# Fused retention and gated feed-forward, one core: the operand sums of the first seven-product tile in another order and on one engine

## Chip, core and metric

The kernel runs on one core of a Trainium2 chip. The core has a matrix engine (TensorE, PE in the profile, with its weight loads as PEld), VectorE (DVE), ScalarE (ACT), GpSimd (POOL) and SyncE (SP), which here only issues DMAs. They run side by side and wait for each other by semaphores. The metric is the time of one execution in microseconds (us) on the device.

## What is computed

Eight batches of eight heads, 576 positions, head size 64. Retention is attention without a softmax, with a decay for each head; its output is then the input of a feed-forward block whose gate is h * cos(h):

```python
scores = scale * np.matmul(q, k.transpose(0, 1, 3, 2))
Dmat = np.where(rel >= 0, gamma[:, None, None] ** rel[None, :, :], 0.0)
attn = np.matmul(scores * Dmat, v)              # (8, 8, 576, 64)
x = attn.transpose(0, 2, 1, 3).reshape(4608, 512)
h = x @ w_in                                    # (4608, 2048)
out = (h * np.cos(h)) @ w_out                   # (4608, 512)
```

## The kernel before

**Tokens and tiles.** The 4608 tokens are cut twice. Retention works on 36 groups of 128 tokens (g). The feed-forward part works on ten tiles of 512, 256, 256 and then seven times 512 tokens (n); tile 3 is the first of the seven (`S7 = 3`), it starts at token 1024, and groups 12 to 15 are prepared for tile 4 while tile 3 runs.

**Retention of a group.** `load` (L105) has SP fetch q, k and v of a group into five buffers each. `prep` (L131) has GpSimd multiply q and k by powers of the decay (L140) and cast v (L155). `transposes` (L163) has SP transpose the result by DMA (L166, into qkT). `scores` (L186) makes q times k on TensorE for one group in a PSUM tile of two banks, tagged "a" or "b", and VectorE multiplies it by the causal mask into `ret` (L206). `states` (L247) multiplies k by v for the state that is carried from group to group; VectorE adds it to the state so far (L284, L286), ScalarE or VectorE casts it (L277). `attn_out` (L292) adds the group's own part (L332) and the carried part (L318) in bank "m", and ScalarE copies that to the next tile's input xT (L349).

**Feed-forward, first half.** `mm1` (L353) makes one block of h on TensorE (L364) in a PSUM tile "a", "b" or "m". ScalarE makes the cosine (L372), VectorE the product gT (L373). In tile 3 a block is 4 of the 16 slices of 128 hidden units by 256 tokens, so there are 8 blocks; `blocks` (L763 to L766) has their order: the first 256 tokens with slices 0, 4, 8, 12, then the second 256 tokens with the same. The later tiles have blocks of 2 slices by 512 tokens.

**Feed-forward, second half.** From tile 3 on, gT times w_out is a 2 x 2 product of quarters with seven instead of eight multiplications (`mm2_seven`, L507). `product` (L469) makes each from 16 matmuls (L497), in the order 1, 2, 6, 4, 7, 5, 3. Products 1, 2 and 4 read gT itself. Products 5, 6, 7 and 3 read sums gs5, gs6, gs7, gs3 of quarters of gT (L437), where gs6 is made from gs5 and gs3 from gs6. Each sum has 8 slices; a sum over 4 of them is an instruction of 128x1024, one over 8 of 128x2048. gs5, gs6 and gs3 are made on VectorE, gs7 on GpSimd in pieces of 2 slices (L435). `sums_after` (L444) puts some of them behind a block of `mm1`; `late_sums` (L463) makes the rest between products. The results are copied (L521) and added (L517) and stored by SP (L527); the adds and stores that a product leaves behind wait in the list `pend` until the next `flush`. A store calls `feed` (L579), which lets GpSimd, SP and the loads go on with later groups.

**Order around the change.** The order of instructions on each engine is written out by hand; an engine works through its own in order. In tile 3, retention work stands ahead of three of the products (`at`, L818 to L823): ahead of product 6 the `flush` and the scores of groups 12 and 13 (`scores2`, L734, banks "a" and "b"); ahead of product 5 `unit7` (L750) with states in bank "st", the output of groups 12 and 13 and the scores of 14 and 15; ahead of product 3 `unit7` with states in bank "b" and the output of groups 14 and 15. After product 1 VectorE makes the rest of gs5 and all of gs6 (`late_sums(n, (5, 6))`, L546), and after the scores ahead of product 6 all of gs3 (L541). `states` has a form `apart` (L254) for a bank "b", in which the two groups' states lie in the two banks of the tile. Tile 4 begins with blocks in the banks a, b, m.

Of the kernel before, what the change touches and what calls it, by code (L numbers as in the profile page):

```python
# [17 lines left out]
def kernel(  # L18
# [16 lines left out]
    nc = tc.nc  # L35
# [21 lines left out]
    S7 = 3  # L57
# [189 lines left out]
    def states(gs, bank="st"):  # L247

        gs = [g for g in gs if g < NG and g % PER != PER - 1]
        if not gs:
            return lambda: (lambda *_: None)
        apart = bank == "b"  # L254
        if apart:
            two = psum.tile([P, 2, 2, HG, D], F32, tag=bank, name="st")
            ps = two[:, :, 0]
        else:
            ps = psum.tile([P, len(gs), HG, D], F32, tag=bank, name="st")
        for x, g in enumerate(gs):  # L260
            qks, vb, qkT, qT = tiles["a", g]
            vs = v_odd[:, g // PER % 2] if g % PER == MIX else vb
            for hg in range(HG):
                for he in range(2):
                    nc.tensor.matmul(  # L265
                        ps[he * D : he * D + D, x, hg, :],
                        lhsT=qks[:, 1, 2 * hg + he, :],
                        rhs=vs[:, head(he, hg), :],
                        start=((apart or x == 0) and hg == 0),
                        stop=((apart or x + 1 == len(gs)) and hg == HG - 1),  # L270
                        skip_group_check=True,
                    )

        def copy(run=nc.vector.tensor_copy):
            for g in gs:
                s, sb = tiles.pop(("s32", g)), blocks4[g % 4]
                run(sb, s)  # L277
                tiles["sb", g + 1] = sb

        def add():  # L280
            for x, g in enumerate(gs):
                s = stp.tile([P, HG, D], F32, tag="s32", name="s32")
                if g % PER in (0, MIX):
                    nc.vector.tensor_copy(s, ps[:, x])  # L284
                else:
                    nc.vector.tensor_tensor(out=s, in0=ps[:, x], in1=tiles["s32"], op=ALU.add)  # L286
                tiles["s32"] = tiles["s32", g] = s
            return copy

        return add  # L290
# [129 lines left out]
    def g_sum(n, x, e0, e1):  # L420

        gT = tiles["g", n]

        def quarter(r, c):
            return gT[:, c * E2 : (c + 1) * E2, r * 256 : (r + 1) * 256]

        if ("gs", n, x) not in tiles:
            tiles["gs", n, x] = sump.tile([P, E2, 256], BF16, tag=f"gs{x}", name=f"gs{x}")
        a, b, op_ = {
            5: lambda: (quarter(1, 0), quarter(1, 1), ALU.add),  # L430
            6: lambda: (tiles["gs", n, 5], quarter(0, 0), ALU.subtract),
            7: lambda: (quarter(0, 0), quarter(1, 0), ALU.subtract),
            3: lambda: (quarter(0, 1), tiles["gs", n, 6], ALU.subtract),
        }[x]()
        eng, step = (nc.gpsimd, 2) if x == 7 else (nc.vector, e1 - e0)  # L435
        for e in range(e0, e1, step):
            eng.tensor_tensor(  # L437
                out=tiles["gs", n, x][:, e : e + step],
                in0=a[:, e : e + step],
                in1=b[:, e : e + step],  # L440
                op=op_,
            )

    def sums_after(n, i):  # L444

        if n == S7:
            if i < 2:
                w_sums(7, i * 4, i * 4 + 4)
            elif i in (4, 5):
                g_sum(n, 7, i % 4 * 4, i % 4 * 4 + 4)  # L450
            elif i == 6:
                g_sum(n, 5, 0, 4)
            return
        for x, e0, e1 in {
            2: ((7, 0, 4),),
            3: ((5, 0, 4),),
            4: ((6, 0, 4), (7, 4, 6)),
            5: ((3, 0, 4),),
            6: ((5, 4, 6), (7, 6, E2)),
        }.get(i, ()):  # L460
            g_sum(n, x, e0, e1)

    def late_sums(n, xs):  # L463
        for x in xs:
            first_part = n == S7
            e0 = {5: 4 if first_part else 6}.get(x, 0 if first_part else 4)
            g_sum(n, x, e0, E2)

    def product(n, x):  # L469
# [37 lines left out]
    def mm2_seven(n, at):  # L507

        s0 = starts[n] // P
        pend = []  # L510

        def flush():
            while pend:
                pend.pop(0)()

        def add(out_, in0, in1):
            return lambda: nc.vector.tensor_tensor(out=out_, in0=in0, in1=in1, op=ALU.add)  # L517

        def copied(tag, x):
            t = op.tile([P, 2, N2], F32, tag=tag, name="ot")  # L520
            nc.scalar.copy(t, tiles["all", x])  # L521
            return t

        def store(t, r, c, s):
            def go():
                r0 = starts[n] + r * 256
                nc.sync.dma_start(  # L527
                    out[r0 : r0 + 256, c * N2 : (c + 1) * N2].rearrange("(j p) c -> p j c", p=P),
                    t,
                )  # L530
                feed(s)

            return go

        for x in (1, 2, 6, 4, 7, 5, 3):
            if x in at:
                at[x](flush, pend)
            else:
                flush()
            if x == 6:  # L540
                late_sums(n, (3,))  # L541
            parts = product(n, x)
            if x == 1:
                c11 = copied("a", 1)
                if 2 not in at:
                    late_sums(n, (5, 6))  # L546
            elif x == 2:
                pend[:0] = [add(c11, c11, tiles["all", 2]), store(c11, 0, 0, s0)]
            elif x == 6:
                u1 = copied("b", 1)  # L550
            elif x == 4:
                c21 = copied("c", 4)
            elif x == 7:
                c22 = copied("d", 1)
                pend += [add(c21, c21, tiles["all", 1]), store(c21, 1, 0, s0 + 1)]
            elif x == 5:
                pend += [
                    add(c22, c22, tiles["all", 5]),
                    add(u1, u1, tiles["all", 5]),
                    store(c22, 1, 1, s0 + 2),  # L560
                ]
            elif n < last:
                pend += [add(u1, u1, tiles["all", 3]), store(u1, 0, 1, s0 + 3)]
                flush()
            else:
                flush()
                for (j, c0, c1), ps in zip(parts, tiles["o", 3]):
                    add(u1[:, j, c0:c1], ps, u1[:, j, c0:c1])()
                    r0 = starts[n] + j * P
                    nc.sync.dma_start(out[r0 : r0 + P, N2 + c0 : N2 + c1], u1[:, j, c0:c1])  # L570
# [189 lines left out]
    for n, w in enumerate(widths):  # L760

        if n in (0, 3):
            halves = [(h, et) for et in range(0, ET, 4) for h in range(2)]  # L763
            if n == 3:
                halves.sort()
            blocks = [(et, half * 256, 256) for half, et in halves]  # L766
        elif n == 1:
            blocks = [(et, half * P, P) for half in range(2) for et in (0, 8)]
        else:
            m = 1024 // w  # L770
            blocks = [(et, 0, w) for et in range(0, ET, m)]
            if n > S7:
                blocks = [(e + k * E2, 0, w) for e in range(0, E2, m) for k in range(2)]
# [14 lines left out]
        g = starts[n] // P + w // P  # L788
# [12 lines left out]
        elif n == 1:  # L801
            todo = pair(6, "ab", 16, 27)
        elif n == 2:
            todo = [(11, lambda: scores2(g)), (25, lambda: unit(g, "m", soon=True))]
            late += [lambda: unit(g + 2, "b", False)]
        else:
            at = {}
            if n + 1 < len(widths):

                def sums_then(then):  # L810
                    late_sums(n, (5, 6))
                    then()

                at = {
                    2: lambda then, off: unit7(g, "st", True, lambda: sums_then(then), off),
                    5: lambda then, off: unit7(g + 2, "st", True, then),
                }
                if n in (3, 4):  # L818
                    at = {
                        6: lambda then, off: (then(), scores2(g)),  # L820
                        5: lambda then, off: unit7(g, "st", True, then),
                        3: lambda then, off: unit7(g + 2, "b", n > 3, then),
                    }  # L823
            mm2_seven(n, at)
            continue
# [43 lines left out]
```

## Time and profile before

| | |
|---|---|
| median of 3 runs | 301.47 us (300.87 to 301.82) |
| the profiled execution | 301.3 us |
| its span, first to last instruction | 299.6 us |
| mean granted TensorE clock | 0.991 |
| TensorE busy | 286.9 us (96% of the span) |
| VectorE busy | 215.1 us (72%) |
| ScalarE busy | 134.1 us (45%) |
| GpSimd busy | 138.9 us (46%) |
| moved by DMA | 50.29 MB, mean 168 GB/s |

A row of the timeline tells start, length, engine, line, operation, tiles written and read, and shapes; a number in brackets is how long the engine stood idle before it, and who ended that. Rows of one kind that follow each other are merged (x16). Two rows of one engine can overlap by about 0.08 us, as an instruction's end is pipelined with the next one's start. A window row has the stretch, each engine's busy time in it with its number of instructions, the granted clock as a share of full speed, the DMA engines' busy share and GB/s. In the waits list a row has the total, the number of waits and the longest.

### The profile page before, as it was taken

The page shows a single profiled execution, that of the slowest core. Times are in us where ns is not written, and L with a number is a line of the kernel's source. Part 1 is how long each engine was busy: PE and PEld are TensorE (multiplying, and loading weights), DVE is VectorE, ACT ScalarE, POOL GpSimd, SP SyncE. Part 2 cuts the span into 40 slices and gives each one's busy share as a digit, 9 for nine tenths or more (in the row PEclk, how much of TensorE's full clock was granted, in tenths as well). Part 3 has the DMA queues.
Part 4 walks back from the last instruction along what each step waited for, and adds up shares of the span by engine and source line. Part 5 has one row for each costly group of instructions (what it writes and reads, how often), then busy time and mean ns, then how long its engine had stood idle before and what let it go on. Part 6 is the DMA issues. An engine that isn't in the chain of part 4 may idle for free.

```text
span 299.6 us, 7314 instructions
## 1 busy us (share of the span) xinstructions
PE 286.9 (96%) x3105; PEld 196.5 (66%) x3105; DVE 215.1 (72%) x262; ACT 134.1 (45%) x163; POOL 138.9 (46%) x151
## 2 busy tenths in 40 slices
PE   7899999999999878999999999999999999999994
PEld 3478647848478757547854785488548854884584
DVE  6776717664568986599678966896689669925943
ACT  3556333515245314553355542644364445525620
POOL 2750067436345797473863791379238113101410
PEclk9999999999999979999999999999999999999998
DMA  8999999999999999997999999996960250011013
GB/s 210 214 210 207 209 217 194 218 210 237 202 170 227 209 242 222 201 233 165 213 216 247 199 218 206 194 234 160 209 117 3 79 135 0 31 51 63 0 37 106
DMA packets 154305, 50.29 MB, mean 168 GB/s; under 512 B 140832, under 2 KB 153248, under 8 KB 154272
## 3 DMA queue, kind: packets, MB, share of 16 engines
q1 hardware_dynamic: 149504, 45.10, 78.9%
q0 software_dynamic: 4224, 4.19, 8.4%
q8 instruction: 24, 0.39, 0.6%
q10 hardware_dynamic: 544, 0.52, 0.5%
q14 instruction: 9, 0.07, 0.1%
HBM read 36.70 MB, written 9.44 MB: 154 GB/s over the span
## 4 chain that ended last, share of the span: by engine, by line
PE 54%; DVE 5%; ACT 1%; issue 0%; DVEq 0%
PE h L364 25%; PE o L497 24%; DVE gT L373 2%; PE ov L332 1%; PE sc L194 1%; PE st L265 1%; PE ov L318 1%; DVE gs L437 1%; DVE ot L517 1%; DVE ret L206 1%; ACT cosh L372 0%; DVE s L286 0%; ACT ot L521 0%; DVEq L864 0%; DVEq L517 0%
## 5 line engine op out<-in xcount | busy, mean ns | idle before, releaser
L364 PE MATMUL h<-xT,w_in_sb 128*128 128x512 bf16 (+2 forms) x832 | 127.6, 314 | 0.8 <-DVE xT L349 0.7
L373 DVE TENSOR_TENSOR gT<-h,cosh 128x1024 bf16<-128x1024 f32 x72 | 88.0, 1223 | 37.3 <-ACT cosh L372 37.2
L372 ACT ACTIVATE cosh<-h,half_pi 128x1024 f32<-128x1024 f32 x72 | 80.2, 1114 | 66.7 <-PE h L364 66.0
L364 PEld LDWEIGHTS <-w_in_sb 128*128 128x128 bf16 x832 | 75.7, 98 | 50.0 <-issue 1.3
L437 POOL TENSOR_TENSOR gs<-gT 128x512 bf16<-128x512 bf16 x28 | 36.0, 1293 | 78.7 <-DVE gT L373 78.7
L140 POOL TENSOR_TENSOR qks<-fq,gq 128x512 bf16<-128x512 f32 x32 | 35.0, 1092 | 48.8 <-DMA fq<-in_q_dram 48.6
L497 PEld LDWEIGHTS <-gs 128*128 128x128 bf16 x456 | 44.0, 99 | 9.4 <-DVE gs L437 3.1
L140 POOL TENSOR_TENSOR qks<-fk,gk 128x512 bf16<-128x512 f32 x35 | 38.6, 1104 | 9.7 <-DMA fk<-in_k_dram 9.1
L206 DVE TENSOR_TENSOR ret<-sc,tri 128x1024 bf16<-128x1024 f32 x32 | 38.1, 1218 | 2.7 <-PE sc L194 2.7
L521 ACT COPY ot<-o 128x512 f32<-128x512 f32 x28 | 16.4, 586 | 45.7 <-PE o L497 44.6
L497 PEld LDWEIGHTS <-gT 128*128 128x128 bf16 x336 | 32.5, 98 | 6.0 <-DVE gT L373 0.6
L497 PE MATMUL o<-ws,gs 128*128 128x256 bf16 x224 | 28.4, 283 | 2.9 <-DVE gs L437 2.9
L517 DVE TENSOR_TENSOR ot<-ot,o 128x512 f32<-128x512 f32 x34 | 22.6, 682 | 11.0 <-ACT ot L521 7.9
L381 PE MATMUL o<-w_out_sb,gT 128*128 128x512 bf16 x128 | 30.1, 380 | 0.0
L497 PE MATMUL o<-w_out_sb,gs 128*128 128x256 bf16 (+1 forms) x232 | 26.8, 269 | 0.0
L497 PE MATMUL o<-w_out_sb,gT 128*128 128x256 bf16 x224 | 26.5, 273 | 0.3 <-DVE gT L373 0.3
L155 POOL CAST vb<-fv 128x512 bf16<-128x512 f32 x32 | 20.9, 652 | 8.3 <-DMA fv<-in_v_dram 7.7
L349 ACT CAST xT<-ov 128x1024 bf16<-128x1024 f32 (+1 forms) x18 | 16.5, 917 | 14.7 <-PE ov L318 12.6
L381 PEld LDWEIGHTS <-gT 128*128 128x128 bf16 x128 | 11.8, 98 | 12.5
L437 DVE TENSOR_TENSOR gs<-gT 128x512 bf16<-128x512 bf16 (+1 forms) x20 | 13.4, 672 | 0.3
L497 PE MATMUL o<-ws,gT 128*128 128x256 bf16 x112 | 13.4, 272 | 0.0
L391 ACT COPY ot<-o 128x512 f32<-128x512 f32 x8 | 4.7, 588 | 17.8 <-PE o L381 17.8
(69 smaller groups left out, 178.9 us busy)
## 6 DMA issues: line engine op xcount, KB each, us to landing
out_dram<-ot SPq DMA_DIRECT2D x35, 256.0 KB, 3.7
fk<-in_k_dram SPq DMA_DIRECT2D x32, 256.0 KB, 4.9
fv<-in_v_dram SPq DMA_DIRECT2D x32, 256.0 KB, 5.2
fq<-in_q_dram SPq DMA_DIRECT2D x30, 256.0 KB, 4.7
w_in_sb<-in_moe_w_in_dram POOLq DMA_DIRECT2D x4, 512.0 KB, 9.1
w_out_sb<-in_moe_w_out_dram POOLq DMA_DIRECT2D x4, 512.0 KB, 16.3
fq<-in_q_dram SPq DMA_DIRECT2D x8, 128.0 KB, 3.7
fk<-in_k_dram SPq DMA_DIRECT2D x8, 128.0 KB, 4.4
```

The lines of the kernel that those rows point to most:

```text
L140: eng.tensor_tensor(out=qks[:, m].rearrange("p (b a) d -> p a b d", a=2), in0=f.rearrange("p (a b) d -> p a b d", a=2), in1=by[:, c, :].re ...
L155: nc.gpsimd.tensor_copy(vb, fv)
L206: nc.vector.tensor_tensor(out=ret.rearrange("p a b i -> p (a b) i"), in0=ps.rearrange("p a b i -> p (a b) i"), in1=mask.unsqueeze(1).to_br ...
L349: evac(tiles["x", n][:, :, t0 : t0 + len(gs) * P], ps.rearrange("p c x i -> p c (x i)"))
L364: nc.tensor.matmul(ps[:, j, :], lhsT=w_in_sb[:, dg, (et + j) * P : (et + j + 1) * P], rhs=xT[:, dg, c0 : c0 + w], start=(dg == 0), stop=(d ...
L372: nc.scalar.activation(cosh, ps, ACTF.Sin, bias=half_pi, scale=1.0)
L373: nc.vector.tensor_mul(gT[:, et : et + m, c0 : c0 + w], ps, cosh)
L381: nc.tensor.matmul(ps, lhsT=gT[:, et, tsi * P : (tsi + 1) * P], rhs=w_out_sb[:, et, :], start=(et == 0), stop=(et == ET - 1),)
L437: eng.tensor_tensor(out=tiles["gs", n, x][:, e : e + step], in0=a[:, e : e + step], in1=b[:, e : e + step], op=op_,)
L497: nc.tensor.matmul(dst[i], lhsT=lhs[:, e, j * P : (j + 1) * P], rhs=rhs[:, e, c0:c1], start=(fresh and e == 0 and (i == 0 or len(parts) > 2)),
L517: return lambda: nc.vector.tensor_tensor(out=out_, in0=in0, in1=in1, op=ALU.add)
L521: nc.scalar.copy(t, tiles["all", x])
```

## The change

It touches tile 3 (and, in one function, the states' banks):

- the second 256 tokens' blocks are made in the order of slices 0, 8, 4, 12 instead of 0, 4, 8, 12;
- gs7 of tile 3 is made on VectorE, its first half behind the fifth block, its second half ahead of the scores that precede product 6; in the later tiles it stays on GpSimd;
- the first half of gs5 is made behind the sixth block instead of the seventh, the first half of gs6 behind the seventh; the second halves of both are made after product 1, where before the second half of gs5 and all of gs6 were made;
- gs3 of tile 3 goes to the next `flush`, ahead of product 4, instead of standing ahead of product 6; it is still one instruction;
- the states ahead of product 3 of tile 3 are made in bank "a" instead of "b", with the two groups apart as in "b".

```diff
-        apart = bank == "b"
+        apart = bank in "ab"
...
-        eng, step = (nc.gpsimd, 2) if x == 7 else (nc.vector, e1 - e0)
+        eng, step = (nc.gpsimd, 2) if x == 7 and n > S7 else (nc.vector, e1 - e0)
...
-            elif i in (4, 5):
-                g_sum(n, 7, i % 4 * 4, i % 4 * 4 + 4)
-            elif i == 6:
-                g_sum(n, 5, 0, 4)
+            elif i in (4, 5, 6):
+                g_sum(n, {4: 7, 5: 5, 6: 6}[i], 0, 4)
...
-            e0 = {5: 4 if first_part else 6}.get(x, 0 if first_part else 4)
+            e0 = 0 if first_part and x == 3 else 6 if x == 5 and not first_part else 4
...
-            if x == 6:
+            if x == 6 and n > S7:
                 late_sums(n, (3,))
...
-                halves.sort()
+                halves.sort(key=lambda u: (u[0], u[0] * (u[1] % 8), u[1]))
...
+                def before_p6(n, then, off):
+                    then()
+                    if n == S7:
+                        late_sums(n, (7,))
+                    scores2(g)
+                    if n == S7:
+                        off.append(lambda: late_sums(n, (3,)))
...
-                        6: lambda then, off: (then(), scores2(g)),
+                        6: lambda then, off: before_p6(n, then, off),
                         5: lambda then, off: unit7(g, "st", True, then),
-                        3: lambda then, off: unit7(g + 2, "b", n > 3, then),
+                        3: lambda then, off: unit7(g + 2, "ab"[n > S7], n > S7, then),
```

## Prediction, made before the changed kernel had run

> **What bounds the kernel now.** I read the page first, then the waits, then the timelines of tile 3 (span 80 to 122), then the granted clock by stretch. The page says that TensorE is the bound:
>
> ```profile
> PE 286.9 (96%) x3105; PEld 196.5 (66%) x3105; DVE 215.1 (72%) x262; ACT 134.1 (45%) x163; POOL 138.9 (46%) x151
> ```
>
> So only time in which TensorE stands, or runs slowly, can be won. The waits list names two such places in reach of the diff:
>
> ```profile
> PE o L497 <- DVE gs L437: 2.9, 1, 2.9
> ...
> PE st L265 <- DVE ret L206: 1.2, 2, 0.8
> ```
>
> The first is product 6 of tile 3, which waits for the operand sum gs6. TensorE's timeline has both (start, length, and in brackets the idle time before):
>
> ```profile
> 103.19 0.64 PE L194 MATMUL sc<-qkT 64*64 64x128 bf16 x32
> 106.73 3.50 PE L497 MATMUL o<-ws,gs 128*128 128x256 bf16 x16 [2.90 <-DVE gs L437]
> ...
> 117.93 0.44 PE L265 MATMUL st<-vb,qks 128*64 128x64 bf16 x16 [0.79 <-DVE ret L206]
> ```
>
> Product 6 then takes 3.33 (106.73 to product 4's start at 110.06) where the product after it takes 1.75 (110.06 to 111.81). The stretches say why (columns: length, TensorE busy, ..., granted clock):
>
> ```profile
> 103.18:106.59 3.41, 0.65 (x33) 0.48 (x32) 3.38 (x2) 0.00 (x0) 3.41 (x3) 1.00 1.31 222
> 106.59:110.00 3.41, 3.27 (x16) 2.34 (x17) 3.41 (x5) 0.00 (x0) 3.41 (x4) 0.50 1.26 262
> 110.00:113.41 3.41, 3.41 (x33) 3.06 (x32) 1.21 (x1) 1.17 (x2) 3.41 (x4) 1.00 1.27 251
> ```
>
> After a stretch of 3.41 us with only 0.65 busy, the next ran at a clock of 0.50. The stall's whole price is 2.90 + (3.33 - 1.75) = 4.48 us. The Trainium skill, in TensorE: Matmul & The Clock Gate, "Why this matters for your kernels", puts the fall of the clock behind idle gaps over about 3 us; the gap here is 2.90, and the trace has the fall all the same. By that sentence the 1.58 would not belong to this gap, and the forecast's gain of 2.4 would be about 0.8; the measured clock decides.
>
> Why gs6 is late stands in VectorE's and GpSimd's timelines:
>
> ```profile
> 100.46 1.45 DVE L437 TENSOR_TENSOR gs<-gT 128x1024 bf16<-128x1024 bf16 x1
> 101.83 1.21 DVE L373 TENSOR_TENSOR gT<-h,cosh 128x1024 bf16<-128x1024 f32 x1
> 103.08 1.50 DVE L437 TENSOR_TENSOR gs<-gT 128x1024 bf16<-128x1024 bf16 x1
> 104.62 2.05 DVE L437 TENSOR_TENSOR gs<-gs,gT 128x2048 bf16<-128x2048 bf16 x1
> ```
>
> ```profile
> 96.90 1.04 POOL L140 TENSOR_TENSOR qks<-fk,gk 128x512 bf16<-128x512 f32 x1 [0.16 <-DMA fk<-in_k_dram]
> 99.64 0.61 POOL L155 CAST vb<-fv 128x512 bf16<-128x512 f32 x1 [1.70 <-DMA fv<-in_v_dram]
> 100.21 5.38 POOL L437 TENSOR_TENSOR gs<-gT 128x512 bf16<-128x512 bf16 x4
> 105.55 2.02 POOL L140 TENSOR_TENSOR qks<-fq,gq 128x512 bf16<-128x512 f32 x1
> ```
>
> The same VectorE sum (128x1024) takes 0.68 at 133.05, where GpSimd is idle at its start. Beside GpSimd's four pieces of gs7 it takes 1.45 and 1.50, and GpSimd's multiplication at 105.55 takes 2.02 instead of 1.04 beside gs6. They take turns: a sum that meets a running GpSimd instruction starts when that one ends and then needs about 0.55 (1.08 for the double size). The multiplications by cos (1.21 to 1.23) show no such thing.
>
> **The change part by part.** Names: gT4 to gT7 are the four multiplications of the second half, a and b a sum's halves.
>
> *Order of blocks.* Same blocks, same banks, same 1.75 pitch of TensorE. Cost nothing; it lets gs5a follow the second of them instead of the third.
>
> *Sums.* GpSimd loses gs7 (5.38); VectorE gains gs7a and gs7b (0.68 each alone, up to 1.6 behind a GpSimd instruction). GpSimd does not fill the hole: its next load, fq of group 16, is issued at 99.64 and lands 3.6 later (103.2); fk lands at 104.6, fv at 105.7, fq and fk of group 17 at 107.0 and 108.2. VectorE's queue then, with steps of 1.17 to 1.25 per multiplication and about 0.6 per sum: gT4 95.71; gs7a from 96.97, behind GpSimd's 96.90 to 97.94, until 98.5; gT5 to 99.6; gs5a from 99.66, behind the cast that ends at 100.25, until 100.8; gT6 to 101.9; gs6a, GpSimd idle, to 102.7; gT7 to 103.8; gs5b from 103.84, behind group 16's fq (103.35 to 104.4), until 104.9; gs6b behind fk (until 105.8), until 106.4. TensorE: product 2 ends at 103.2, scores of the first group run, those of the second need gT7's bank (103.9, a wait of 0.4); product 6's first half runs 104.2 to 105.1 on gs6a, then waits 1.3 for gs6b. That the halves are waited for apart is taken from product 7, whose weight loads already follow GpSimd's four pieces one by one; were it not so, 0.9 more would go. Product 6 ends at 107.3 instead of 110.06: 2.8 won of 4.48. The one near tie is at 96.9: if gs7a goes first (0.07 us decide), gs5a misses the cast too, gs6b ends near 103.9 and all 4.48 is won.
>
> *gs7b and gs3 behind.* After gs6b stand the add of c11 (0.60), gs7b (0.6), two masks (2.3) and gs3 (1.2): about 111.1. Product 7 needs gs7b at about 109.9, it is there by 107.7 (108.7 behind a GpSimd instruction). The state adds, next in the queue, become ready at 111.3. No DMA moves: the store of c11 and the loads and transposes fed with it stand on SP ahead of these sums, before and after. So this part costs nothing, with 0.2 to spare; each further wait for GpSimd (1.0) would move the adds and the masks behind them.
>
> *States in bank a.* They wait for the mask of bank a, 1.14 earlier than that of b; but attn_out, next on TensorE, needs the second mask after 0.5 more. Of the wait of 0.79 some 0.3 remains: 0.5 won. Tile 4's first block needs that bank back after product 3 (1.85): hidden. So tile 4 starts 3.3 earlier, at 117.7.
>
> *What is late next.* Two things. First, tile 4: GpSimd's preparation of groups 20 and 21 is tied to loads (123.18 to 129.2) and does not move, while VectorE's sums do. Each meets GpSimd once more often; a meeting costs up to 1.0, VectorE has no slack there (1.14 + 0.60 of a pitch of 1.73), and tile 4's first product already waits 0.27 for gT6. Played through with the same turn-taking, gT6 ends at 134.1 instead of 136.6: 2.5 left of 3.3, and for 1.8 to 2.5 at the start about 1.3. Second, transposes of group 23:
>
> ```profile
> 160.48 1.06 SPq L527 DMA_DIRECT2D out_dram<-ot  x1
> 161.64 1.39 SPq L166 DMA_TRANSPOSE qkT<-qks  x1
> ...
> DMA to landing us min/median/max: 5.0/5.0/5.0
> ```
>
> SP's queue is full without a hole from 99 to 178: the store at 160.48 carries data that was added by 151.2. So that transpose still lands at 161.64 + 5.0 = 166.6, and its scores now start at 169.46 (second half of the scores at 169.20). Beyond 2.8 us TensorE would wait there. Later ones have 4 us or more, and after 178 SP waits for VectorE and moves along.
>
> **Sum.** 2.8 + 0.5 - 0.9 (tile 4) = 2.4, under the cap of 2.8. The profiled execution took 301.3 (span 299.6), so 298.9; the runs' median is 301.47, so **299.1**.
>
> The Trainium skill, in Perfetto Trace Analysis, "Optimizing Scalar/DVE Operations", warns that moving work between GPSIMD and VectorE might not help, as they share a port. The rows agree that they block each other, but the piece of 5.38 becomes two of 0.68; by that sentence alone only the bank's 0.5 would be won.
>
> **The rivals.**
> 1. *Half the clock again, or more turns lost.* In the case above TensorE is busy about 1.7 of a stretch of 3.41; the trace shows 0.65 leading to the half clock and 2.62 (116.83 to 120.24) not, so 1.7 is open. With it product 6's rest and product 4 cost up to 1.7 more; 1.6 to 1.8 is won at tile 4's start, 1.3 after it: 300.2.
> 2. *Everything is won.* gs7a goes first, and group 23's transpose lands earlier, as DMA finds other gaps: 4.48 less 0.3: 297.3. Against it: SP's full queue.
> 3. *The change does not do it:* the halves are waited for whole, and gs3 pushes the masks back by as much as was won; the wait only moves to L206 and to tile 4. Near 301.2.
> 4. *Slower: VectorE's queue.* If a GpSimd instruction stood ready at each of the seven sums (1.5 to 1.6 each, gs3 2.1), gs6b would end at 108.5, gs3 at 115.1, against 114.1 for the state adds now, and the mask before product 3 would be 1.0 later than today: about 302.4. It decides once the sums lose over some 5 us in all. Against it: GpSimd has no data between 100.25 and 103.2.
>
> **Chances and range.** Forecast (298.6 to 299.7) 0.52; rival 1 (299.8 to 300.5) 0.24; rival 2 0.09; rival 3 0.10; rival 4 0.05. Faster by over 0.3% (0.9 us, about what a measurement here can tell from no change): 0.85; within: 0.10; slower: 0.05. The range leaves out rival 4, most of 2 and most of 3: 298.2 to 300.7.
>
> **What would show it.** Right: no GpSimd row at L437 before tile 4; product 6 starting near 104.2 in two parts, around a gap of 0 to 1.4; clock 1.00 after it; the wait of L265 for L206 at or under 0.3; tile 4's blocks 2.6 to 3.4 earlier; a wait in its first product of about 1. Wrong: product 6 in one piece after gs6b, a second stretch at 0.50, gs3 ending after the states' matmuls, or scores of group 23 that wait for a transpose far before or after 166.6.

## The result, and the profile after

| | before | changed |
|---|---|---|
| median | 301.64 us (300.87 to 302.23, 4 runs) | 298.51 us (298.26 to 298.70, 4 runs) |
| ratio, with 95% interval | | 0.9897 (0.9873 to 0.9922) |
| the profiled execution | 301.3 us, span 299.6 | 298.52 us, span 296.8 |
| its mean granted clock | 0.991 | 0.999 |

The changed kernel is 3.1 us faster; 2.4 were forecast. Medians and ranges below take in all executions; the ratios leave disturbed ones out, of the kernel before too.

TensorE's timeline of the changed kernel over tile 3 (start, length, idle before in brackets; where the new lines shift the code, L497 is now L495):

```profile
100.03 3.66 PE L495 MATMUL o<-w_out_sb,gT 128*128 128x256 bf16 x32
103.62 0.64 PE L194 MATMUL sc<-qkT 64*64 64x128 bf16 x32
104.19 1.92 PE L495 MATMUL o<-ws,gs 128*128 128x256 bf16 x16
105.95 1.91 PE L495 MATMUL o<-ws,gT 128*128 128x256 bf16 x16
...
113.82 0.41 PE L332 MATMUL ov<-ret,vb 128*64 128x128 bf16 x8 [0.20 <-DVE ret L206]
```

Product 6 follows the scores at once: the idle 2.90 is gone, and its 16 matmuls take 1.76 to product 4's start. The wait of 0.79 for the second mask is one of 0.20, now in attn_out. VectorE's and GpSimd's rows show why, and that it was close:

```profile
97.40 0.69 DVE L437 TENSOR_TENSOR gs<-gT 128x1024 bf16<-128x1024 bf16 x1
...
103.58 0.69 DVE L437 TENSOR_TENSOR gs<-gs,gT 128x1024 bf16<-128x1024 bf16 x1
```

```profile
97.44 1.55 POOL L140 TENSOR_TENSOR qks<-fk,gk 128x512 bf16<-128x512 f32 x1
99.80 0.62 POOL L155 CAST vb<-fv 128x512 bf16<-128x512 f32 x1 [0.81 <-DMA fv<-in_v_dram]
104.03 1.14 POOL L140 TENSOR_TENSOR qks<-fq,gq 128x512 bf16<-128x512 f32 x1 [3.61 <-DMA fq<-in_q_dram]
```

The first half of gs7 starts at 97.40 and takes 0.69; GpSimd's multiplication starts 0.04 later and takes 1.55 instead of 1.04, so it is GpSimd that waits. gs6's second half (103.58) is there before product 6 needs it.

What was won is partly given back 60 us later, in tile 5, where the scores of group 23 wait for their transpose:

```profile
164.87 0.39 PE L194 MATMUL sc<-qkT 64*64 64x128 bf16 x16
166.60 0.42 PE L194 MATMUL sc<-qkT 64*64 64x128 bf16 x16 [1.34 <-DMA qkT<-qks]
```

The issue of that transpose on SP's queue, and its time to landing:

```profile
162.15 1.54 SPq L166 DMA_TRANSPOSE qkT<-qks  x1
...
DMA to landing us min/median/max: 4.4/4.4/4.4
```

The same, as stretches. First the changed kernel, cut at the starts of product 1 and product 4 of tile 3, and of tiles 4, 5 and 6 (columns: length, then busy times, granted clock, DMA):

```profile
100.03:105.95 5.92, 5.92 (x82) 5.08 (x80) 5.85 (x8) 1.70 (x2) 2.25 (x3) 1.00 1.17 232
105.95:116.27 10.32, 10.12 (x194) 8.55 (x192) 9.54 (x12) 5.00 (x9) 7.47 (x8) 1.00 1.10 234
116.27:148.14 31.87, 30.58 (x353) 19.91 (x352) 25.82 (x29) 14.18 (x17) 19.27 (x20) 1.00 1.14 210
148.14:179.11 30.97, 29.53 (x335) 19.94 (x337) 24.20 (x29) 14.49 (x18) 21.87 (x22) 1.00 1.03 220
```

and the kernel before, cut at the same places:

```profile
99.60:110.06 10.46, 7.56 (x82) 5.91 (x80) 10.36 (x9) 1.70 (x2) 10.42 (x9) 0.84 1.23 255
110.06:120.86 10.80, 10.01 (x194) 8.57 (x192) 6.90 (x10) 5.00 (x9) 7.80 (x9) 1.00 1.15 222
120.86:152.47 31.61, 30.65 (x355) 20.07 (x352) 24.63 (x29) 14.20 (x17) 19.44 (x21) 1.00 0.98 204
152.47:181.91 29.44, 29.44 (x337) 19.88 (x337) 23.91 (x29) 14.50 (x18) 18.97 (x19) 1.00 1.22 225
```

Won: 4.54 up to product 4, 0.48 in the rest of tile 3. Lost: 0.26 in tile 4, 1.53 in tile 5, and the changed kernel's product 1 happened to start 0.43 later. 4.54 + 0.48 - 0.26 - 1.53 - 0.43 = 2.80, the difference of the spans (299.6 - 296.8); after tile 6's start both take 117.7.

### The profile page after: what moved, and what is told of

It is laid out like the page before. It is cut to its first block, busy times and chain, and to the rows that moved or that the text cites. A ratio compares the mean times of both kernels' runs of the same rounds, so it can differ in the third digit from the quotient of the medians.

```text
span 296.8 us, 7293 instructions
## 1 busy us (share of the span) xinstructions
PE 285.0 (96%) x3083; PEld 195.9 (66%) x3105; DVE 215.4 (73%) x265; ACT 133.9 (45%) x163; POOL 133.7 (45%) x147
## 4 chain that ended last, share of the span: by engine, by line
PE 80%; DMA 8%; DVE 6%; SPq 2%; issue 1%; ACT 1%; POOL 0%; DVEq 0%
PE h L364 39%; PE o L495 26%; PE o L381 7%; DMA qkT<-qks 4%; DMA fk<-in_k_dram 2%; DMA w_in_sb<-in_moe_w_in_dram 2%; PE sc L194 2%; PE ov L332 2%; DVE gT L373 2%; PE ov L318 2%; DVE gs L437 1%; SPq L117 1%; PE st L265 1%; DVE ot L515 1%; DVE ret L206 1%
## 5 line engine op out<-in xcount | busy, mean ns | idle before, releaser
L437 POOL TENSOR_TENSOR gs<-gT 128x512 bf16<-128x512 bf16 x24 | 30.6, 1282 | 69.0 <-DVE gT L373 69.0
L140 POOL TENSOR_TENSOR qks<-fq,gq 128x512 bf16<-128x512 f32 x32 | 33.6, 1052 | 60.8 <-DMA fq<-in_q_dram 56.4
L495 PEld LDWEIGHTS <-gs 128*128 128x128 bf16 x456 | 43.1, 98 | 5.8
L140 POOL TENSOR_TENSOR qks<-fk,gk 128x512 bf16<-128x512 f32 x35 | 39.8, 1138 | 9.4 <-DMA fk<-in_k_dram 8.3
L495 PEld LDWEIGHTS <-gT 128*128 128x128 bf16 x336 | 32.4, 98 | 6.5 <-DVE gT L373 1.1
L519 ACT COPY ot<-o 128x512 f32<-128x512 f32 x28 | 16.4, 585 | 43.2 <-PE o L495 43.2
L381 PE MATMUL o<-w_out_sb,gT 128*128 128x512 bf16 x120 | 28.9, 380 | 0.5 <-issue 0.2
L495 PE MATMUL o<-w_out_sb,gT 128*128 128x256 bf16 x224 | 26.6, 273 | 0.6 <-DVE gT L373 0.5
L495 PE MATMUL o<-ws,gs 128*128 128x256 bf16 x224 | 26.8, 273 | 0.0
L495 PE MATMUL o<-w_out_sb,gs 128*128 128x256 bf16 (+1 forms) x232 | 26.8, 269 | 0.0
L437 DVE TENSOR_TENSOR gs<-gT 128x512 bf16<-128x512 bf16 (+1 forms) x22 | 14.6, 664 | 0.4
L495 PE MATMUL o<-ws,gT 128*128 128x256 bf16 x112 | 13.4, 273 | 0.0
L194 PEld LDWEIGHTS <-qkT 64*64 64x64 bf16 (+1 forms) x512 | 8.9, 105 | 6.5 <-ACT qkT L176 2.3
```

What stands on the lines that cost most here:

```text
L140: eng.tensor_tensor(out=qks[:, m].rearrange("p (b a) d -> p a b d", a=2), in0=f.rearrange("p (a b) d -> p a b d", a=2), in1=by[:, c, :].re ...
L381: nc.tensor.matmul(ps, lhsT=gT[:, et, tsi * P : (tsi + 1) * P], rhs=w_out_sb[:, et, :], start=(et == 0), stop=(et == ET - 1),)
L437: eng.tensor_tensor(out=tiles["gs", n, x][:, e : e + step], in0=a[:, e : e + step], in1=b[:, e : e + step], op=op_,)
L495: nc.tensor.matmul(dst[i], lhsT=lhs[:, e, j * P : (j + 1) * P], rhs=rhs[:, e, c0:c1], start=(fresh and e == 0 and (i == 0 or len(parts) > 2)),
```

## The experiments

The table has one profiled execution of each, by the same stretches, and the times of all executions. Stretches are differences of starts in TensorE's timeline: A from product 1 to product 4 of tile 3, B to tile 4, C tile 4, D tile 5; after it all take 117.7 to 118.0. Product 1 starts at 99.3 to 100.5 everywhere but in experiment 2 (103.12). The kernel before had 21 executions of median 301.48 beside the first four, 26 of 301.08 beside the next four, 21 of 301.22 beside the last four.

| kernel | A | B | C | D | median us (executions) | ratio (95%) |
|---|---|---|---|---|---|---|
| before | 10.46 | 10.80 | 31.61 | 29.44 | 301.64 (4) | |
| changed | 5.92 | 10.32 | 31.87 | 30.97 | 298.51 (4) | 0.9897 (0.9873, 0.9922) |
| 1 changed, transpose early | 5.92 | 10.35 | 32.01 | 29.44 | 298.49 (10) | 0.9897 (0.9862, 0.9933) |
| 2 before, transpose early | 9.70 | 10.88 | 30.93 | 29.44 | 301.27 (12) | 0.9990 (0.9968, 1.0011) |
| 3 changed, bank b | 7.73 | 10.89 | 32.03 | 29.44 | 299.33 (6) | 0.9924 (0.9901, 0.9947) |
| 4 changed, early and bank b | 5.92 | 10.99 | 32.57 | 29.44 | 298.79 (6) | 0.9904 (0.9875, 0.9933) |
| 5 before, idle matmuls | 8.80 | 10.79 | 32.02 | 29.45 | 300.83 (10) | 0.9983 (0.9963, 1.0003) |
| 6 before, bank a alone | 8.25 | 10.32 | 32.39 | 29.44 | 300.69 (10) | 0.9996 (0.9974, 1.0018) |
| 7 changed, gs7 on GpSimd | 7.56 | 10.32 | 32.80 | 29.44 | 298.86 (5) | 0.9938 (0.9912, 0.9964) |
| 8 before, gs7 alone | 9.51 | 12.14 | 31.43 | 29.44 | 300.46 (10) | 0.9981 (0.9944, 1.0018) |
| 9 changed, once more | 5.92 | 10.40 | 31.62 | 29.56 | 298.95 (6) | 0.9891 (0.9849, 0.9933) |
| 10 as 1, once more | 7.22 | 10.32 | 32.08 | 29.44 | 299.61 (10) | 0.9931 (0.9892, 0.9971) |
| 11 before, halves alone | 9.18 | 10.79 | 31.98 | 29.44 | 301.93 (10) | 1.0012 (0.9986, 1.0037) |
| 12 changed, gs6 whole | 6.37 | 10.32 | 32.79 | 29.44 | 298.85 (4) | 0.9897 (0.9850, 0.9944) |

**1. The transpose of group 23 earlier, in the changed kernel.**

```diff
-  ... ((0, 1, 2, 4) if n else (-1, 0, 1, 4))[r]
+  ... ((0, 1 + (n == 1), 2, 4) if n else (-1, 0, 1, 4))[r]
```

> The changed kernel, with the preparation and transpose of group 23 fed one store earlier in tile 4, so that SP issues that transpose ahead of the loads of groups 27 and 28 and of a store. Theory (the won time is capped by that transpose, which landed at 166.56 while its scores stood ready 1.34 us earlier): the wait of 1.34 before those scores goes, and the time falls by about 1.3, to 297.2 us (ratio to before about 0.985). Rival (what is missing is lost in tile 4 or elsewhere on TensorE, and the wait only hides behind it): the wait goes, but others take its place, and the time stays within 0.4 of 298.5.

The transpose landed at 161.4 and the wait is gone: D is 29.44 and the profiled execution took 297.06. Half of the ten executions lie at 297.06 to 297.56, where theory put them, but two at 299.4 to 299.6 and three at 301.3 to 302.6, the latter with a clock of 0.994. The median, 298.49, is where the rival put it, though no other wait took the place of this one in the profile. So the mechanism is shown in the profile, and the gain in the median is not.

**2. The same in the kernel before.**

> The kernel before, with the same earlier transpose of group 23 and nothing else. Theory: before, the transpose landed 2.8 us ahead of its scores, so nothing waits for it and the time stays within 0.3 of before (ratio 1.00). Rival (the earlier transpose helps by itself, or disturbs the loads behind it): a change of 1 us or more either way.

No change (0.9990). The wait that it removes did not exist there. The profiled execution is one of the longest (303.69, clock 0.987), and its product 1 starts 3.5 late: in tile 2 the scores waited 2.06 for a transpose (0.54 in the kernel before), and a stretch at half clock followed.

```profile
84.22 0.42 PE L194 MATMUL sc<-qkT 64*64 64x128 bf16 x16 [2.06 <-DMA qkT<-qks]
```

The edit changes the order of issues in tile 4, which comes later, so it is not what made that wait.

**3. The changed kernel with the states in bank b.**

```diff
-        apart = bank in "ab"
+        apart = bank == "b"
...
-                        3: lambda then, off: unit7(g + 2, "ab"[n > S7], n > S7, then),
+                        3: lambda then, off: unit7(g + 2, "b", n > S7, then),
```

> The changed kernel, with the states before product 3 of tile 3 back in bank b. Theory of the cap: the states wait about 0.6 longer there (0.8 in all, for the second mask), tile 4 starts about 0.5 later, but the wait of 1.34 for group 23's transpose takes it up: 298.5 us, no change from the changed kernel (ratio to before 0.990). Rival (the parts add up): 0.5 slower than the changed kernel, 299.0 us (0.991 to 0.992).

B is 10.89 against 10.32, so the bank's 0.57 is there. The ratio, 0.9924, is nearer to the rival's 0.991 to 0.992 than to 0.990. But it is no test of the cap: the profiled execution lost 1.81 in A, so TensorE came to group 23 later than its transpose. VectorE's and GpSimd's rows show another order than in the changed kernel's profile:

```profile
97.22 1.44 DVE L437 TENSOR_TENSOR gs<-gT 128x1024 bf16<-128x1024 bf16 x1
...
105.23 1.42 DVE L437 TENSOR_TENSOR gs<-gs,gT 128x1024 bf16<-128x1024 bf16 x1
```

```profile
97.07 1.04 POOL L140 TENSOR_TENSOR qks<-fk,gk 128x512 bf16<-128x512 f32 x1 [0.16 <-DMA fk<-in_k_dram]
```

GpSimd's multiplication began 0.15 ahead of gs7's first half. From there four sums take 1.14 to 1.44, gs6 is complete at 106.65 instead of 104.27, and product 6 waits 1.42 in its middle. This is the branch that the prediction had worked out.

**4. Both edits.**

> The changed kernel with group 23's transpose earlier and the states in bank b. Theory: with the cap away the 0.5 of the bank shows at the end: 0.4 to 0.6 slower than the run with the earlier transpose and bank a, so about 297.7 us (ratio to before 0.987). Rival (the bank is hidden for another reason, such as the mask that attn_out needs anyway): no difference between the two.

The profile has A as in the changed kernel (5.92), D without a wait, and B at 10.99. Against experiment 1 the span is 1.43 longer (296.78 against 295.35): 0.64 of it is B, 0.56 is C. So in these two profiles the bank's part shows at the end, where nothing caps it, beside another loss as large; the medians (298.79, 298.49) are too spread to tell.

**5. Idle matmuls in the gap of the kernel before.**

```diff
             if x == 6:
+                if n == S7:
+                    warm(psum.tile([P, 512], F32, tag="m", name="idle"), 12)
                 late_sums(n, (3,))
```

> The kernel before, with 12 idle matmuls of zeros (128x512, 0.21 us each, into a bank that nobody reads then) in the gap before product 6 of tile 3; the gap itself stays, but TensorE is busy in it. Theory (the half clock follows from the idle stretch): product 6 takes 1.75 instead of 3.33 at a clock of 1.00, tile 4 starts 1.6 earlier, and the time falls by 1.0 to 1.6, to 300.0 to 300.6 us, since group 23's transpose does not cap so little. Rival (the half clock has another cause than this gap of 2.9 us): product 6 stays at 3.3 and the time at 301.5.

TensorE's timeline:

```profile
103.92 2.54 PE L184 MATMUL idle<-zeros 128*128 128x512 bf16 x11 [0.16 <-issue]
106.58 1.92 PE L497 MATMUL o<-ws,gs 128*128 128x256 bf16 x16
108.33 1.91 PE L497 MATMUL o<-ws,gT 128*128 128x256 bf16 x16
```

Product 6 still starts 7.05 after product 1 (7.13 before), but takes 1.75 instead of 3.33, so A is 1.66 shorter. So the half clock belongs to the gap. At the end only 0.17% is left (0.5 us, where 1.0 to 1.6 was expected), not told from nothing: C took 0.41 back, and the half clock does not come in every execution of the kernel before. Of its 68 executions beside the experiments, 38 had a mean clock under 0.996; in the three groups these took 1.2, 1.1 and 1.3 us more than the others. All ten with the idle matmuls were at 0.996 or more.

**6. Bank a alone.** The edit of 3, the other way, in the kernel before.

> The kernel before, with only the states before product 3 of tile 3 in bank a. Theory: the wait of 0.79 for the second mask becomes 0.2 to 0.3 in front of attn_out, tile 4 starts 0.5 to 0.6 earlier, and since neither tile 4's turns nor the cap of 2.8 take much of so little, the time falls by 0.1 to 0.6: 300.9 to 301.4 us. Rival (tile 4's first block waits for the states' adds in that bank): no change, or slower.

B is 10.32 against 10.80: 0.48 won in place. (A is 8.25 because this execution waited 2.27 and kept the full clock; that lies ahead of the states.) At the end 0.9996: not told from nothing.

**7. The changed kernel with gs7 back on GpSimd.**

```diff
-        eng, step = (nc.gpsimd, 2) if x == 7 and n > S7 else (nc.vector, e1 - e0)
+        eng, step = (nc.gpsimd, 2) if x == 7 else (nc.vector, e1 - e0)
...
                 g_sum(n, {4: 7, 5: 5, 6: 6}[i], 0, 4)
+                if i == 6:
+                    g_sum(n, 7, 4, E2)
...
-                    if n == S7:
-                        late_sums(n, (7,))
```

> The changed kernel, with gs7 of tile 3 back on GpSimd in its four pieces, each half behind the block that completes it; block order, halves, gs3 and bank a stay as changed. Theory (the turns with GpSimd are what made gs6 late): VectorE's sums meet the four pieces again, gs6's second half ends at about 105.5 to 106.5 instead of 104.3, product 6 waits 1 to 2 us in its middle, tile 4 starts 1 to 2 us later than in the changed kernel; with the cap of 1.34 most of that is hidden, so 298.5 to 299.3 us at the end. Rival (the order and the halves do it all): no gap in product 6 and tile 4 starts as in the changed kernel.

Three sums take 1.51 or 1.52 again, and product 6 stands 1.47 in its middle; tile 4 starts 17.88 after product 1 instead of 16.24.

```profile
105.96 1.05 PE L497 MATMUL o<-ws,gs 128*128 128x256 bf16 x8 [1.47 <-DVE gs L437]
```

At the end the profiled execution took 298.86 against 298.52: the wait for group 23 is gone and covers most of the loss, as expected, and product 1 happened to start 0.74 earlier. The ratios are further apart (0.9938 against 0.9897, intervals that overlap), so up to 1.2 us may be left. All five executions have a clock of 0.997 or more: with a wait of 1.47 instead of 2.90 the clock stays.

**8. gs7 alone moved, in the kernel before.**

```diff
-        eng, step = (nc.gpsimd, 2) if x == 7 else (nc.vector, e1 - e0)
+        eng, step = (nc.gpsimd, 2) if x == 7 and n > S7 else (nc.vector, e1 - e0)
```

> The kernel before, with only gs7 of tile 3 moved from GpSimd to VectorE (two instructions behind the fifth and sixth block); order of blocks, whole gs6, gs3 ahead of product 6 and bank b as before. Theory (the turns with GpSimd are what made gs6 late): without them gs6 ends at about 104.3 instead of 106.7, the wait before product 6 falls from 2.9 to about 0.5, the clock stays at 1.00, and tile 4 starts about 3.9 earlier; the end is capped by group 23's transpose, so 298.5 to 299.2 us. Rival (order and halves are needed): the wait stays over 1.5 us, and the time over 300.

The theory fails here as far as this profile goes. GpSimd's gs7 is gone, and product 6 waits 2.92 as before (the half clock behind it falls mostly on product 4 this time, so B is 12.14):

```profile
97.69 1.27 DVE L437 TENSOR_TENSOR gs<-gT 128x1024 bf16<-128x1024 bf16 x1
...
104.30 1.32 DVE L437 TENSOR_TENSOR gs<-gT 128x1024 bf16<-128x1024 bf16 x1
105.66 1.95 DVE L437 TENSOR_TENSOR gs<-gs,gT 128x2048 bf16<-128x2048 bf16 x1
```

```profile
107.66 2.37 PE L497 MATMUL o<-ws,gs 128*128 128x256 bf16 x16 [2.92 <-DVE gs L437]
```

```profile
97.36 1.04 POOL L140 TENSOR_TENSOR qks<-fk,gk 128x512 bf16<-128x512 f32 x1
...
104.03 1.04 POOL L140 TENSOR_TENSOR qks<-fq,gq 128x512 bf16<-128x512 f32 x1 [3.31 <-DMA fq<-in_q_dram]
105.29 1.23 POOL L140 TENSOR_TENSOR qks<-fk,gk 128x512 bf16<-128x512 f32 x1 [0.21 <-DMA fk<-in_k_dram]
```

The preparation of groups 15 and 16 takes gs7's place as the one that VectorE takes turns with. The ten executions fall into two halves: five at 298.3 to 299.8 (clock 0.997 or more) and five at 301.1 to 302.8 (0.994 or less). The move alone wins in one half and nothing in the other. The profile is one of the second half; where the five fast ones won, no profile shows.

**9. The changed kernel once more,** no edit.

> The changed kernel once more, beside the next three on one chip. Theory (the wait for group 23's transpose takes up what the turns in tile 3 win or lose): its executions lie close together, 298.2 to 299.0 us, all at a clock of 0.997 or more. Rival (the turns of VectorE and GpSimd in tile 3, which were lucky in its profile, decide): executions spread from 298.3 to 300, in step with those of the run with bank b.

The ratio repeats (0.9891). The expected narrow spread does not, and the rival's wider one is nearer: five executions lie at 297.24 to 299.91, all at a clock of 0.997 or more, and a sixth took 305.0 at 0.986. In this profile the transpose of group 23 landed at 165.20, 1.36 earlier than in the first one, and its scores started at 165.24, with hardly a wait: no cap worth naming, D is 29.56, span 295.5. So the cap is real but not fixed: it moves by more than a microsecond from one execution to the next.

**10. The early transpose once more.**

> The changed kernel with group 23's transpose earlier, once more. Theory: most executions at 297.0 to 297.6 us, 1.3 below the changed kernel; the three of ten at 301.3 to 302.6 and a clock of 0.994 were lost ahead of tile 3, in tile 2's wait for a transpose (2.06 us in one profile of another kernel), which every kernel here has, so about as many of the changed kernel's executions show it. Rival (the earlier transpose itself brings them, by pushing loads back): they appear here again and not with the changed kernel, and the median is no better.

Not better than the changed kernel beside it (0.9931 against 0.9891, with intervals that overlap). Three of ten executions are again at a clock of 0.994 (300.9, 301.7, 302.2); of the changed kernel's ten in all, nine are at 0.997 or more and one, the 305.0, at 0.986. Experiment 4, with the same edit, has none in six. With the variants 3, 7 and 12 that makes six of 26 with the earlier transpose and one of 25 without it. That leans to the rival, but weakly, and the late tile 2 of experiment 2 came before the edit could act. No profile caught one of these executions of the changed kernel, so where their time goes, and whether the edit brings it, stays open.

**11. gs6 in halves alone, in the kernel before.**

```diff
-                if 2 not in at:
+                if n == S7:
+                    g_sum(n, 6, 0, 4)
+                    g_sum(n, 5, 4, E2)
+                    g_sum(n, 6, 4, E2)
+                elif 2 not in at:
                     late_sums(n, (5, 6))
```

> The kernel before, with only gs6 of tile 3 made in two halves after product 1, its first half ahead of the second half of gs5; gs7 stays on GpSimd, blocks, gs3 and banks as before. Theory (what counts is that product 6 can start on the first half, since that splits the wait and keeps the clock): product 6's first half starts at about 104.5 to 105.5, a gap of 0.5 to 2 stands in its middle, clock 1.00, product 4 starts 1.5 to 2.5 us earlier than before, and the time falls by 1 to 2, to 299.1 to 300.1 us. Rival (the turns with GpSimd lose as much again, since there is one sum more): 300.5 us or more.

A miss: 1.0012. Four sums now take 1.42 to 1.70 each, each behind a GpSimd instruction, and product 6 waits twice:

```profile
105.77 1.05 PE L497 MATMUL o<-ws,gs 128*128 128x256 bf16 x8 [1.06 <-DVE gs L437]
108.78 1.05 PE L497 MATMUL o<-ws,gs 128*128 128x256 bf16 x8 [1.96 <-DVE gs L437]
```

This profile has the full clock, but it is one of only two executions of ten that do (0.997 and 0.998); the other eight lie at 0.989 to 0.994, and no profile shows where they lost it. So it is not shown that splitting the wait keeps the clock, as the theory had it; the two waits here still add up to 3.02.

**12. The changed kernel with gs6 in one piece.**

```diff
-            elif i in (4, 5, 6):
-                g_sum(n, {4: 7, 5: 5, 6: 6}[i], 0, 4)
+            elif i in (4, 5):
+                g_sum(n, {4: 7, 5: 5}[i], 0, 4)
...
-            e0 = 0 if first_part and x == 3 else 6 if x == 5 and not first_part else 4
+            e0 = 0 if first_part and x in (3, 6) else 6 if x == 5 and not first_part else 4
```

> The changed kernel, with gs6 of tile 3 in one piece after product 1, as before; order, gs7 on VectorE, gs3 and bank a as changed. Theory (the halves are what keeps TensorE going when a turn is lost): product 6 starts in one piece when gs6 ends, 0.5 to 2.7 us after the scores, and in some executions the clock halves; 0.3 to 1.5 slower than the changed kernel, 298.8 to 300 us. Rival (gs7's place and the order do it): as fast as the changed kernel, 298.5.

A is 0.45 longer (product 6 waits 0.39 for the whole), the end is the same: 298.85, ratio 0.9897. With VectorE first at 97.5 the halves are hardly needed. Whether they matter when GpSimd is first, no profile of this kernel shows.

## Why the prediction was right, by its steps

**The price of the stall: right.** 4.48 was read from the trace of before; where the order is favourable A is 4.54 shorter. The half clock's share, 1.58, is shown by experiment 5 (product 6 takes 1.75 instead of 3.33). The prediction took it for a fixed part of the time; by their clocks 38 of 68 executions pay it. By the sentence of the Trainium skill (TensorE: Matmul & The Clock Gate, "Why this matters for your kernels") a gap under 3 us should not have cost the clock; the measurement decides against it.

**The turns of VectorE and GpSimd in tile 3: both branches right, the wrong one taken.** The prediction called 96.9 a near tie and took GpSimd first: product 4 at 7.7 after product 1, with a gap of 1.3 in product 6. Experiments 3 and 10 are that branch: 7.73 and 7.22, gaps of 1.42 and 0.78. The changed kernel's own profile took the other, 5.92. Of the seven profiles with the new order and gs7 on VectorE, five have VectorE first, by 0.04 to 0.26 us (changed, 1, 4, 9, 12: A 5.92 to 6.37), and two GpSimd, by 0.02 and 0.15 (10, 3: A 7.22 and 7.73). Which branch an execution takes is luck as far as the prediction goes. That product 6 waits for the two halves apart, which it took from product 7, was right (the rows of experiments 7 and 11).

**The cause named for gs6's lateness: half of it.** The prediction put it on GpSimd's gs7. Experiment 8 shows that moving gs7 alone leaves the wait at 2.92 in the profiled execution, and experiment 7 that putting it back costs about 1.6 of the 5. What the runs show in its place is two things: when VectorE reaches its last multiplication, and how long the sums between that and gs6 take, each of them longer when it meets a GpSimd instruction, whichever that is. In the kernel before, the multiplication starts 2.23 after product 1 and the sums take 1.50 and 2.05; with gs7 moved alone it is 2.73, then 1.32 and 1.95; with the new order and gs7 on GpSimd 2.30, then 1.51 and 1.52; in the changed kernel 1.57, then 0.69 and 0.69. None of the parts that were tried alone in the kernel before (6, 8, 11) gives an interval clear of no change; every run that has the new order of blocks with gs7 on VectorE, or with gs6 in halves, or both (changed, 1, 3, 4, 7, 9, 10, 12) does. The new order was not run alone, so what it is worth by itself stays open; gs3's new place went along in all of these runs, and VectorE makes gs3 behind the same two masks as before (at 107.91; 109.46 before). The warning of the Trainium skill (Perfetto Trace Analysis, "Optimizing Scalar/DVE Operations") that moving work between the two might not help agrees with half of experiment 8's executions.

**gs7b and gs3 behind: right.** They were to cost nothing, with 0.2 to spare. In the changed kernel's profile VectorE still stood idle for 0.19 before the state adds, though gs3 took 1.93 instead of the 1.2 counted.

**Bank a: right.** 0.5 forecast; 0.48 measured alone (10.80 to 10.32), 0.57 in the changed kernel (10.89 to 10.32, experiment 3).

**Tile 4's turns: right in kind, too large for the profile.** 0.9 of loss entered the sum (the prediction's own working gives 0.8, from 3.3 down to 2.5). C rose by 0.26 in the changed kernel, and by 0.0 to 1.2 against 31.61 in its other variants; the wait in tile 4's first product, forecast at about 1, is 0.48.

**The cap by group 23's transpose: right.** It was forecast to land at 166.6 whatever TensorE does and to limit the gain to 2.8. It landed at 166.56, TensorE waited 1.34, and the spans differ by 2.8. That it is the same place to a tenth is luck: the transpose was issued 0.5 later (162.15, 161.64 before) and took 4.4 instead of 5.0. In the profile experiment 1 removes the wait, and hardly anything else. The fixed place was wrong: the landings in the profiles without the early transpose lie between 163.4 and 167.4.

So that the sum of 2.4 came out close to the profiles' 2.8 is in part luck. Tile 3 won 1.7 more than forecast and tile 4 lost 0.6 less; the transpose took 1.5 of that away, and the later start of product 1 another 0.4. Tile 4 therefore started 4.59 earlier (116.27 against 120.86), outside the 2.6 to 3.4 that the prediction gave as a sign of being right.

## What to carry to other kernels

When a sum on VectorE takes twice its usual time, look at what GpSimd runs in the same moment: the two took turns here, and who began first, by 0.02 to 0.26 us, went with a difference of 1.3 to 1.8 us. Count the work that stands between the last input and the first use, and what it can meet there, and start what can be started before the last input, rather than only moving work from one engine to the other. And before adding up what a removed stall brings, walk along the later waits on the full DMA queue: the first transpose with less slack than the gain can be the lid. Here it took 1.5 of 5 us in one profile of the changed kernel and 0.1 in the other.

## What the runs showed of the hardware

**The clock halves after a stretch that is far from idle.** Granted stretches of half clock last 3.41 us, and stretches before them, cut on the same grid, tell how busy TensorE was. Experiment 8 and experiment 11, two neighbours of the bound:

```profile
105.57:108.98 3.41, 1.32 (x13) 1.19 (x13) 3.38 (x4) 0.00 (x0) 3.40 (x3) 1.00 1.32 224
108.98:112.39 3.41, 3.41 (x19) 2.41 (x17) 2.73 (x3) 0.58 (x1) 2.17 (x4) 0.50 1.28 261
```

```profile
106.89:110.30 3.41, 1.52 (x14) 1.37 (x15) 3.38 (x4) 0.43 (x1) 3.41 (x4) 1.00 1.17 232
110.30:113.71 3.41, 3.41 (x52) 2.91 (x52) 2.97 (x3) 1.09 (x3) 3.41 (x4) 1.00 1.07 234
```

1.32 of 3.41 busy led to a clock of 0.50, 1.52 did not. Four such stretches in mid-span of these profiles were halved after (0.65, 1.28, 1.30 and 1.32 busy, with gaps of 1.95 to 2.76 in them), none with 1.52 or more. The 1.7 that rival 1 of the prediction left open thus lies on the side that kept the clock. The half stretch that ends each profile fits this: it follows one with at most 1.29 busy. The grid lies elsewhere in each execution (an edge at 106.59 in the kernel before, at 108.98 in experiment 8), so the same gap can halve the clock in one and not in another: 2.27 us of idle in experiment 6 lay across an edge and cost nothing, 2.13 in experiment 2 lay within one stretch and cost a half stretch.

**One execution is not the kernel.** Executions of one program spread over 1 to 5 us in most groups here (0.4 at least, 7.8 at most), where the change is worth 3. The half clock, the order of a tie and a late transpose are reasons that the profiles show. Neither of the changed kernel's two profiles has a stretch of half clock in mid-span.
